# A copy in PSUM and a joint addition in the second channel product, a fourth grouped block per batch, and gates ahead of other work, in a gated attention and token-and-channel mixer

## The chip, the cores and the metric

The kernel runs on one core of a Trainium2 chip. The metric is the device time of one execution in microseconds. A core has a matmul engine (TensorE, PE in the profile), a vector engine (VectorE, DVE), a scalar engine (ScalarE, ACT), GpSimd (POOL) and SyncE (SP), which here issues DMAs. [...] Each engine works through its own list of instructions in the order in which the kernel emitted it, and semaphores order the engines against each other.

## The reference

There are 8 batches, 3008 positions (S), 256 channels, 64 columns of z, 256 token-mixing and 1536 channel-mixing hidden units:

```
attn = relu(z zT / S)^2
x    = u * (attn v)
xt   = x transposed (channels x positions)
h    = relu(xt w_tok1) w_tok2
u2   = x + h transposed
out  = u2 + relu(u2 w_ch1) w_ch2
```

All is given and returned in f32; the kernel multiplies in bf16 and accumulates in f32.

## The kernel before

A batch is cut into NQ = 6 blocks of 512 positions (the last has 448). For each block the attention half computes scores (`sc`, L470), relu and square on ScalarE and VectorE, and the product with v (`acc`, L697), which uses half of the rows of the matmul array and takes two accumulators per block half. `finish` (L809) combines them: ScalarE copies one accumulator to `cp` (L825), VectorE adds the other (L831), and `gate` multiplies with u (L851, and L856 for the last 64 positions of the short block) and writes `xT`. The buffers of the tag "res" (three) hold `cp` among others.

The mixer half of a batch has token mixing (`a_ps`, L1058, then `h_ps`, L1128), the residual, the first channel product and the second. The first channel product of a block makes twelve hidden tiles of 128 units; ordinarily each takes two matmuls of 512 columns (`hp`, L1192), and a ReLU of two tiles at once (L1231, 1024 columns). In some blocks the first four hidden tiles come in a seven-product form of a 2 x 2 block product (Strassen and Winograd's), `grouped_ch1` (L1288), in four steps a, b, c, d of 2, 2, 2 and 1 products. It needs sums of quarters of the tokens (`token_quarters`, L1256) and uses one PSUM bank pair `gp`. After step a ScalarE keeps one bank in `s5` (L1323) and copies the other bank over it (L1320); b accumulates on both; after it come a ReLU of half the tile and a second copy; after c VectorE adds both banks to `s5` in one custom instruction (L1338); after d a last ReLU. `grouped` (L1249) says which blocks: those with q of 1 to 3 in batches 1 to 7.

The second channel product of a block is also in seven-product form, `product` (L1421): products k = 1 to 7 of twelve 128-column matmuls each (six in the short last block of a batch), over tiles of hidden units and sums of them (`hsum`, L1383 to L1401). Before the change product 1 and then 6, 7 and 4 go to one bank of the pair `xb`, and 2, 5 and 3 to the banks of a second pair `zb`. Products 2, 6, 7, 4 and 3 go on top of an earlier one where the form asks for it. After each product VectorE adds the bank, with the residual `u_sb` where a quarter of the result opens, to the result tile `ro` (L1480): seven additions of 128 x 256 per block. The very last block of the kernel takes the plain form (`ch2`).

The order of all this work is written out when the kernel is built. The work alternates between attention stages and mixer stages, since attention uses half of the array's rows and the rest uses all of them; mixer stage j holds blocks 3 to 5 of one batch and 0 to 2 of the next. Within a mixer stage the pieces of a block stand in a written order: a tuple such as `GROUPED` (L1024), `ORDER_LAST` (L1026) or the plain one at L1673, where a letter is a step of the next block's group, a number other than 0 a product, and 0 the next ordinary piece of the first channel product. A planner (`next_piece`, L1690; `run_engines`, L388; `push`, L369) walks along these orders, keeps an estimated time for each engine, and emits each engine's operations when, by its estimate, they are ready. `push(engine, ready, busy, latency, ...)` puts an operation into an engine's waiting list, `room` and `needs` hold it back until buffers or other operations are there, and `first` ranks it.

Of the kernel before, what the change touches and what calls it, by code (L numbers as in the profile page):

```python
# [26 lines left out]
class Sooner:  # L27
# [5 lines left out]
    @property  # L33
    def t(self):
        return None if self.done.t is None else self.done.t - self.us


# [21 lines left out]
def kernel(  # L59
# [749 lines left out]
    def finish(blk, dh, end):  # L809


        W, acc = blk.W, blk.acc[dh]
        summed = Done()
        guess[blk.home[dh]] = end + 1.7
        ring.append((summed, blk.home[dh]))

        def load(e):
            return max(free[e], end) + sum(op.busy for op in waiting[e])

        on_act = blk.b > 0 or load("act") + 0.46 < load("dve") + 0.67  # L820

        def copy(t):
            cp = sb.tile([P, QW], F32, tag="res", name="cp", bufs=3)
            if on_act:
                nc.scalar.copy(cp[:, :W], acc[:, 1, :W])  # L825
            else:
                nc.vector.tensor_copy(cp[:, :W], acc[:, 1, :W])
            push("dve", t, 0.66, 0.78, lambda t: add(cp, t), first=1, done=summed)

        def add(cp, t):  # L830
            nc.vector.tensor_add(cp[:, :W], acc[:, 0, :W], cp[:, :W])  # L831
# [7 lines left out]
    gated = [0]  # L839

    def gate(blk, dh, acc, t):
        b, q, W = blk.b, blk.q, blk.W
        uT = uTs[b, q]
# [179 lines left out]
    BORROW = 3  # L1023
    GROUPED = ("a", 0, 1, 2, "b", 6, 5, 0, "c", 7, 3, 0, 4, "d")  # L1024
    VERY_LAST = (B - 1, NQ - 1, CHT // 2 - 1)
    ORDER_LAST = ((1, 2, 6, 5, 7, 0, 3, 4), (1, 2, 6, 5, 0, 7, 3, 0, 4))  # L1026

    def add_mixer(b):
# [150 lines left out]
        def ch1(q, c2, borrowed, end):  # L1179
# [48 lines left out]
            def evacuate(t):  # L1228
# [12 lines left out]
            engine, busy = ("act", 0.92) if on_act else ("dve", 1.15)  # L1241
# [12 lines left out]
        g_done = {(q, d, k): Done() for q in range(NQ) for d in range(CHT // 4) for k in range(3)}  # L1254

        def token_quarters(q):  # L1256
# [5 lines left out]
            def first_two(t):  # L1262
                live["xT"] += 2
                tile_["T"] = sb.tile(
                    [P, 4, 2 * P], BF16, tag="xT", name="t_sums", bufs=ROOM["xT"])
                st["T", q] = tile_["T"]
                st["s5", q] = sb.tile([P, QW], F32, tag="xT", name="s5", bufs=ROOM["xT"])
                nc.vector.tensor_sub(tile_["T"][:, 0:2], quarter[:, :, 1], quarter[:, 0])
                push("dve", t - 0.1, 0.27, 0.4, third)
# [10 lines left out]
            def begin(t):  # L1280
                push("dve", t, 0.4, 0.53, first_two, room=lambda: live["xT"] < ROOM["xT"] - 1)

# [5 lines left out]
        def grouped_ch1(q, d, stage, end):  # L1288
# [41 lines left out]
            def relu_last(t):  # L1330
                nc.scalar.activation(h[:, 1, 0], half(1), ACT.Relu)  # L1331
                recent[0] = h[:, 1, 0, :1]
                live["xT"] -= 2
                if ("rest", q, d) in st:
                    st.pop(("rest", q, d))(t)
# [79 lines left out]
        def bank_of(q, k):  # L1415

            if k in (2, 5, 3):
                return st["zb", q][:, int(k != 2)]
            return st["xb", q][:, 0]

        def product(q, k, end):  # L1421
# [6 lines left out]
            if k == 2:  # L1428
                st["z_slot", q], _ = take_slot()
                st["zb", q] = bank_pair(st["z_slot", q], "zb")  # L1430
# [20 lines left out]
            if k == 4:  # L1451
                done_with_h2(q)
                for d in range(CHT // 4):
                    release(home_of(q), [1], end + 0.2)
            collect(q, k, end)

        def collect(q, k, end):
# [9 lines left out]
            def us(m, h):  # L1467
                return st["u", q][:, h, m * n:m * n + n, :]

            blocks_of = {1: (0, 0), 2: (0, 0), 5: (1, 1), 6: (1, 0), 3: (1, 0), 7: (1, 1),  # L1470
                         4: (0, 1)}
            opening = k in (1, 5, 6, 4)

            def add(t):
                if k == 1:
# [3 lines left out]
                m, h = blocks_of[k]  # L1479
                nc.vector.tensor_add(  # L1480
                    res(m, h), source, us(m, h) if opening else res(m, h))
                recent[0] = st["res", q][:, 0, :1]
                over[q] -= 1
# [8 lines left out]
            done = taken[q, k]  # L1492
            if k == 1:
                with_u(q, ready, lambda at: push(
                    "dve", at, busy, busy + 0.15, add, first=1, room=(home_of(q),),
                    frees=frees_of(q), done=done))
            else:
                done = push("dve", ready, busy, busy + 0.15, add, first=1, done=taken[q, k],
                            room=lambda: ("res", q) in st)
            if k == 3:  # L1500
# [3 lines left out]

        over = [7] * NQ
        us_uses = [[1] for _ in range(NQ)]
# [134 lines left out]
        def add_product(q, k):  # L1641
            needs = {
                1: [Sooner(h2_done[q, c], 0.111 * c) for c in range(CHT // 2)] + w_done[2:],
                2: [], 5: [mix_done, taken[q, 2]], 6: [taken[q, 1]], 3: [taken[q, 5]], 7: [taken[q, 6]],
                4: [taken[q, 7]]}[k]
            kind = {5: 0, 7: 1, 6: 2, 4: 3}.get(k)
            if kind is not None:
                needs = needs + [Sooner(s_done[q, d, kind], 0.222 * d) for d in range(CHT // 4)]
            if q == NQ - 1 and k == 5 and b % 2 == 0:
                needs = needs + [tok1_over[b + 1]]  # L1650
            cost = pairs_of(q) * (CHT // 2) * column_time(P)
            tails.append(Piece(cost, needs, lambda end: product(q, k, end), opens=k == 1,
                               closes=k == 4, key=(b, 2 + q), slot=k in (1, 2),
                               joins=k == 1 and q == NQ - 1))
# [8 lines left out]
        for q in range(NQ):  # L1663
# [5 lines left out]
            if fast(q):  # L1669
                us_uses[q][0] += bool(rest)  # L1670
                h2_uses[q] += bool(rest)
                for k in (ORDER_LAST[b % 2] if q == NQ - 1 else GROUPED if grouped(q + 1) else
                          (0, 0, 1, 2, 0, 6, 5, 0, 7, 3, 0, 4)):  # L1673
                    if isinstance(k, str):
# [415 lines left out]
```

## Time and profile before

| | us |
|---|---|
| median of 3 runs | 1110.19 |
| the runs | 1110.31, 1108.81, 1110.19 |
| the profiled execution | 1109.13 |
| its span, first to last instruction | 1107.3 |

| engine | busy us | instructions |
|---|---|---|
| TensorE, matmuls | 1102.2 | 11199 |
| VectorE | 811.5 | 1791 |
| ScalarE | 684.7 | 906 |
| GpSimd | 168.2 | 386 |

The granted TensorE clock is 1.000 over the whole span. In the timeline a row gives the start in us from the span's start, the length in us, the engine, the line, the operation with out<-in, the shape and how many instructions it covers. Matmuls are pipelined: the printed end of a row lies behind the start of the next, so lengths of matmul work are read from start to start. In the grouped rows the number behind "x" is the count, then the busy time in us and the mean length in ns, and then the idle time of that engine just before them and what ended it.

The stage borders, by the matmuls of the timeline, are at 127.3 (mixer), 164.8 (attention), 198.3 (mixer), 267.3 (attention), 335.2 (mixer), 403.5 (attention), 471.4 (mixer), and so on with mixer stages beginning at 606.2, 742.5, 877.5 and 1011.3.

### The profile page before, as it was taken

How to read it: one execution, taken by the hardware profiler on the slowest of the kernel's cores; microseconds unless marked ns; L12 is line 12 of the kernel's file. 1: busy time of each engine (PE TensorE's matmuls, PEld its weight loads, DVE VectorE, ACT ScalarE, POOL GpSimd, SP SyncE). 2: the span in 40 equal slices, each digit the busy share in tenths (PEclk: the TensorE clock that was granted, in tenths of full speed). 3: DMA queues.
4: the chain of work that ended last, by engine and by line, in shares of the span. 5: the costliest groups of instructions: out<-in, count | busy, mean ns of one | idle time of the engine just before them, and what ended most of it. 6: DMA issues, size and time to landing. Idle time of an engine off the chain costs nothing.

```text
span 1107.3 us, 27459 instructions
## 1 busy us (share of the span) xinstructions
PE 1102.2 (100%) x11199; PEld 695.2 (63%) x11199; DVE 811.5 (73%) x1791; ACT 684.7 (62%) x906; POOL 168.2 (15%) x386
## 2 busy tenths in 40 slices
PE   9999999999999999999999999999999999999998
PEld 3444575776557665576656865557755677556776
DVE  6889865886758866578766796567966778656785
ACT  7999555646854567546665467663776537743464
POOL 5320110321003110032100320003210120000100
PEclk9999999999999999999999999999999999999999
DMA  9999947798978969789896796977989778684222
GB/s 179 167 199 184 149 96 152 127 179 146 190 127 149 190 133 177 127 156 191 140 189 120 133 218 141 170 122 150 198 160 169 116 145 185 125 160 104 64 59 96
DMA packets 465726, 165.55 MB, mean 150 GB/s; under 512 B 433024, under 2 KB 448960, under 8 KB 465600
## 3 DMA queue, kind: packets, MB, share of 16 engines
q1 hardware_dynamic: 436208, 131.11, 58.9%
q0 software_dynamic: 28880, 32.32, 21.5%
q8 instruction: 87, 1.43, 0.6%
q14 instruction: 39, 0.32, 0.1%
q10 hardware_dynamic: 512, 0.38, 0.1%
HBM read 65.40 MB, written 24.64 MB: 81 GB/s over the span
## 4 chain that ended last, share of the span: by engine, by line
PE 99%; DVE 0%; ACT 0%; issue 0%
PE acc L697 42%; PE hp L1192 19%; PE xb L1447 11%; PE zb L1447 8%; PE sc L470 6%; PE h_ps L1128 4%; PE a_ps L1058 3%; PE gp L1312 3%; PE op L1544 2%; PE first_acc L614 1%; PE wp L210 0%; DVE at L516 0%; ACT at L508 0%; DVE zr L183 0%; PE first_acc L189 0%; DVE zT L1850 0%
## 5 line engine op out<-in xcount | busy, mean ns | idle before, releaser
L697 PEld LDWEIGHTS <-v_sb 64*128 64x128 bf16 x4418 | 245.7, 94 | 212.5 <-issue 1.3
L1231 ACT ACTIVATE h2pre<-hp 128x1024 bf16<-128x1024 f32 (+1 forms) x245 | 239.9, 1005 | 182.7 <-PE hp L1192 180.5
L697 PE MATMUL acc<-at,v_sb 64*128 64x512 bf16 (+1 forms) x2738 | 341.6, 374 | 0.0
L508 ACT ACTIVATE at<-sc 128x1024 bf16<-128x1024 f32 (+1 forms) x290 | 286.8, 1027 | 72.0 <-PE sc L470 66.4
L516 DVE TENSOR_TENSOR at<-at 128x1024 bf16<-128x1024 bf16 (+1 forms) x290 | 198.1, 687 | 112.1 <-ACT at L508 107.9
L1192 PE MATMUL hp<-xT,w_ch_sb 128*128 128x512 bf16 (+1 forms) x984 | 238.3, 374 | 0.0
L697 PE MATMUL acc<-fl,v_sb 64*128 64x512 bf16 (+1 forms) x1680 | 193.0, 367 | 0.0
L1192 PEld LDWEIGHTS <-w_ch_sb 128*128 128x128 bf16 x984 | 90.8, 98 | 79.0 <-issue 2.6
L1447 PEld LDWEIGHTS <-hsum 128*128 128x128 bf16 x2088 | 127.9, 98 | 19.6 <-issue 0.5
L470 PE MATMUL sc<-zT 64*128 64x512 bf16 (+1 forms) x732 | 132.4, 359 | 0.1
L1383 DVE TENSOR_TENSOR hsum<-h2pre 128x1024 bf16<-128x1024 bf16 (+1 forms) x141 | 90.0, 647 | 22.7 <-ACT h2pre L1231 12.6
L825 ACT COPY cp<-acc 128x512 f32<-128x512 f32 (+1 forms) x94 | 54.9, 584 | 79.9 <-PE acc L697 69.0
L831 DVE TENSOR_TENSOR cp<-acc,cp 128x512 f32<-128x512 f32 (+1 forms) x94 | 63.4, 675 | 54.8 <-ACT cp L825 54.0
L1447 PEld LDWEIGHTS <-h2pre 128*128 128x128 bf16 x1566 | 93.8, 98 | 10.0
L496 ACT ACTIVATE at<-sc 128x512 bf16<-128x512 f32 (+3 forms) x152 | 56.2, 450 | 29.2 <-PE sc L470 28.8
L1447 PE MATMUL xb<-shared_sb,hsum 128*128 128x128 bf16 x1044 | 73.6, 219 | 0.0
L1480 DVE TENSOR_TENSOR ro<-xb,u_sb 128x256 f32<-128x256 f32 (+1 forms) x141 | 56.3, 400 | 17.9 <-PE xb L1447 17.7
L470 PEld LDWEIGHTS <-zT 64*128 64x128 bf16 x732 | 42.4, 94 | 41.6 <-issue 3.8
L129 POOL CAST mark<-at 128x1 f32<-128x1 bf16 x24 | 9.3, 386 | 388.1 <-DVE at L516 388.1
L851 DVE TENSOR_TENSOR xT<-cp,uT 128x512 bf16<-128x512 f32 (+1 forms) x94 | 62.4, 663 | 0.8
L547 DVE TENSOR_TENSOR at<-at 128x512 bf16<-128x512 bf16 (+3 forms) x152 | 41.0, 320 | 23.8 <-ACT at L496 23.8
L1401 DVE TENSOR_TENSOR hsum<-h2pre,hsum 128x512 bf16<-128x512 bf16 (+1 forms) x141 | 55.1, 400 | 4.1 <-ACT h2pre L1331 2.5
(107 smaller groups left out, 1114.8 us busy)
## 6 DMA issues: line engine op xcount, KB each, us to landing
out_dram<-ro SPq DMA_DIRECT2D x40, 512.0 KB, 3.2
v_sb<-in_v_dram POOLq DMA_DIRECT2D x40, 256.0 KB, 4.6
ur<-in_u_dram POOLq DMA_DIRECT2D x40, 256.0 KB, 5.0
w_tok_sb<-in_moe_w_tok_dram POOLq DMA_DIRECT2D x10, 256.0 KB, 10.5
shared_sb<-in_z_dram POOLq DMA_DIRECT2D x35, 64.0 KB, 4.2
at<-at SPq DMA_TRANSPOSE x114, 2.4
out_dram<-ro SPq DMA_DIRECT2D x7, 256.0 KB, 3.7
fl<-at SPq DMA_TRANSPOSE x105, 4.5
```

Of the source, the lines that this page charges most:

```text
L470: nc.tensor.matmul(sc[:, r, c0:c1], zT[h, k:k + P], zT[h, m + c0:m + c1], start=True, stop=True)
L496: nc.scalar.activation(a3[:, i, c0:c1], sc[:, r, c0:c1], ACT.Relu, scale=inv_S)
L508: nc.scalar.activation(view, sv, ACT.Relu, scale=inv_S)
L516: nc.vector.tensor_mul(view, view, view)
L697: nc.tensor.matmul(o, vs[blk.b, g][rows, i, dh * P:(dh + 1) * P], rhs, start=(dh, h) not in blk.begun, stop=stop, skip_group_check=True)
L831: nc.vector.tensor_add(cp[:, :W], acc[:, 0, :W], cp[:, :W])
L851: nc.vector.tensor_mul(xT[:, dh, :full * P].rearrange("p (t s) -> p t s", s=P), acc[:, :full * P].rearrange("p (t s) -> p t s", s=P), uT[: ...
L1192: nc.tensor.matmul(hps[r % len(hps)][:, r, :W], w_ch1_sb[:, dc, cc * P:(cc + 1) * P], xT[:, dc, :W], start=(dc == 0), stop=(dc == DT - 1))
L1231: nc.scalar.activation(h2[:, :, :W], hp[:, :, :W], ACT.Relu)
L1383: nc.vector.tensor_sub(sums["s"][:, 0:2, :, :n * P], h[:, :, 1], h[:, 0])
L1447: nc.tensor.matmul(to[:, i * P:(i + 1) * P], lhs, weights[:, c2, :], start=(first_use and c2 == 0 and i == 0), stop=(c2 == CHT // 2 - 1), ...
L1480: nc.vector.tensor_add(res(m, h), source, us(m, h) if opening else res(m, h))
```

## The change

There are three parts.

1. In the second channel product, product 1 now goes to bank 1 of `xb`, and ScalarE copies this bank to bank 0 (a new `fork`). Product 2 accumulates on bank 0, and 6, 7 and 4 accumulate on bank 1, so both quarters of the result that take product 1 have it in PSUM. The pair `zb` is taken at product 5 and holds only 5 and 3. VectorE adds after 5, 6, 7 and 3 as before, and after 4 once for both banks of `xb` with the residual, so a block has five additions, the last twice as wide. Product 2 now needs the copy, and the planner is told to put it behind the additions of 6 and 7; the written orders are changed to match.
2. `grouped` holds for one more block, q = 4, in batches 1 to 6. Its token sums and `s5` cannot lie in an `xT` buffer, so they share one of the six buffers of `h2`; they are made during block 3 of the mixer stage before (`LATE_T`), and lie there over the attention stage that comes between. The mixer stage that then follows opens with step a of this group, product 1 of block 3, an ordinary piece, step b. `GROUPED` becomes one order per block.
3. `gate` is ranked 0.12 us earlier in the planner's list, and the copies of the accumulators are counted, so that at most three buffers of "res" are planned as held. One estimate, that of the ReLU on ScalarE (`RELU`), is 0.95 for 0.92.

By the order of instructions there are 84 more `gp` matmuls of 256 columns and 48 fewer `hp` matmuls of 512; 47 more copies on ScalarE; 62 fewer instructions on VectorE; 18 of the 198 ReLUs of 1024 columns leave ScalarE, six of which go to VectorE. GpSimd and SyncE keep their instructions, and the DMAs stay as they are.

```diff
@@ finish / gate
         def copy(t):
+            copies[0] += 1
             cp = sb.tile([P, QW], F32, tag="res", name="cp", bufs=3)
...
-            push("dve", t, 0.58, 0.7, lambda t: gate(blk, dh, cp, t), first=1,
+            push("dve", t - 0.12, 0.58, 0.7, lambda t: gate(blk, dh, cp, t), first=1,
...
-        push(engine, end + 0.21, busy, busy + 0.15, copy, first=1)
+        push(engine, end + 0.21, busy, busy + 0.15, copy, first=1,
+             room=lambda: copies[0] + live["us"] < 3)
...
     def gate(blk, dh, acc, t):
+        copies[0] -= not blk.whole
@@ orders
-    GROUPED = ("a", 0, 1, 2, "b", 6, 5, 0, "c", 7, 3, 0, 4, "d")
+    LATE_T = 4
+    RELU = 0.95
+    GROUPED = (('a', 0, 1, 0, 'b', 2, 6, 5, 'c', 7, 3, 0, 'd', 4), ('a', 0, 1, 0, 'b', 2, 6, 5, 'c', 7, 3, 0, 'd', 4), (0, 'a', 0, 1, 0, 'b', 2, 6, 5, 'c', 7, 3, 0, 'd', 4), ('a', 1, 0, 'b', 6, 0, 5, 'c', 2, 3, 7, 'd', 0, 4), ('a', 0, 1, 0, 'b', 6, 2, 5, 'c', 7, 0, 3, 'd', 4), ('a', 0, 1, 0, 'b', 6, 2, 5, 'c', 7, 0, 3, 'd', 4), ('a', 0, 1, 0, 'b', 6, 2, 5, 'c', 7, 0, 3, 'd', 4))
+    PLAIN = (0, 1, 0, 5, 2, 6, 0, 0, 7, 0, 3, 4)
-    ORDER_LAST = ((1, 2, 6, 5, 7, 0, 3, 4), (1, 2, 6, 5, 0, 7, 3, 0, 4))
+    ORDER_LAST = ((1, 2, 6, 5, 7, 0, 3, 4), (1, 6, 0, 5, 2, 0, 3, 7, 4))
@@ the group
-            if c2 == (3 if q else 0) and q + 1 < NQ and grouped(q + 1):
+            if c2 == (0, 3, 3, LATE_T if b < B - 1 else 3)[min(q, HALF)] and q + 1 < NQ and grouped(q + 1):
                 token_quarters(q + 1)
...
-            return b > 0 and 0 < q <= HALF and d == 0
+            return b > 0 and 0 < q <= HALF + (b < B - 1) and d == 0
...
+                else:
+                    live["h2"] += 1
+                    kept = sb.tile([P, 2, QW], F32, tag="h2", name="t_s5", bufs=ROOM["h2"])
+                    tile_["T"] = kept[:, 0].bitcast(BF16).rearrange("p (k n) -> p k n", k=4)
+                    st["s5", q] = kept[:, 1]
@@ the products
-            if k in (2, 5, 3):
-                return st["zb", q][:, int(k != 2)]
-            return st["xb", q][:, 0]
+            if k in (5, 3):
+                return st["zb", q][:, 0]
+            return st["xb", q][:, int(k != 2)]
...
-            first_use = k in (1, 2, 5)
+            first_use = k in (1, 5)
...
+            if k in (2, 6, 7, 4):
+                behind = [taken[q, j] for j in (1, 6, 7)]
+                for op in waiting["dve"]:
+                    if op.done in behind:
+                        op.ready = max(op.ready, end + 0.21)
...
+            def fork(t):
+                nc.scalar.copy(bank_of(q, 2)[:, :n * P], bank_of(q, 1)[:, :n * P])
...
+                if k == 4:
+                    nc.vector.tensor_add(
+                        st["res", q][:, :n, :].rearrange("p i (h d) -> p h i d", d=P),
+                        st["xb", q][:, :, :n * P].rearrange("p h (i d) -> p h i d", d=P),
+                        st["u", q][:, :, :n, :])
+                else:
+                    m, h = blocks_of[k]
+                    nc.vector.tensor_add(
+                        res(m, h), source, us(m, h) if k in (5, 6) else res(m, h))
...
             if k == 1:
+                push("act", ready, busy, busy + 0.15, fork, first=2, done=done)
+            elif k == 2:
+                pass
+            elif begins:
...
-        over = [7] * NQ
+        over = [5] * NQ
@@ needs
-                2: [], 5: [mix_done, taken[q, 2]], 6: [taken[q, 1]], 3: [taken[q, 5]], 7: [taken[q, 6]],
+                2: [taken[q, 1]], 5: [mix_done], 6: [taken[q, 1]], 3: [taken[q, 5]], 7: [taken[q, 6]],
                 4: [taken[q, 7]]}[k]
+            if k == 2:
+                needs = needs + [Read(taken[q, j]) for j in (6, 7)]
```

More of the change, by code (lines that the diff above doesn't have):

```diff
@@ L35, in t, with __init__ @@
         return None if self.done.t is None else self.done.t - self.us
+class Read:
+    def __init__(self, done):
+        self.done = done
+    @property
+    def t(self):
+        return self.done.t or 0.0
 class Op:
@@ L1497, in collect @@
             else:
-                done = push("dve", ready, busy, busy + 0.15, add, first=1, done=taken[q, k],
-                            room=lambda: ("res", q) in st)
+                us_ = busy if k != 4 else 0.62 if n == 2 else 0.34
+                push("dve", ready, us_, us_ + 0.15, add, first=1, done=done,
+                     room=lambda: ("res", q) in st)
             if k == 3:
@@ L1671, in add_mixer @@
                 h2_uses[q] += bool(rest)
-                for k in (ORDER_LAST[b % 2] if q == NQ - 1 else GROUPED if grouped(q + 1) else
-                          (0, 0, 1, 2, 0, 6, 5, 0, 7, 3, 0, 4)):
+                for k in (ORDER_LAST[b % 2] if q == NQ - 1 else GROUPED[q + (b == B - 1) * (HALF + 1)] if grouped(q + 1) else
+                          PLAIN):
                     if isinstance(k, str):
```

44 lines of the change are left out of this document (26 added, 18 removed).

## The prediction

> **What bounds the kernel now.** I read the page's busy shares and its chain first, then TensorE's own waits, then a table of three stages, then single stretches of the timeline.
>
> ```profile
> span 1107.3 us, 27459 instructions
> PE 1102.2 (100%) x11199; PEld 695.2 (63%) x11199; DVE 811.5 (73%) x1791; ACT 684.7 (62%) x906; POOL 168.2 (15%) x386
> PE 99%; DVE 0%; ACT 0%; issue 0%
> ```
>
> ```profile
> PE wp L210 <- DVE zero L1735: 1.2, 1, 1.2
> PE first_acc L614 <- DVE at L516: 0.4, 1, 0.4
> ```
>
> ```profile
> 335.15:403.49 68.34, 68.34 (x759) 50.94 (x758) 56.74 (x142) 37.61 (x47) 17.04 (x40) 1.00 0.86 159
> 403.49:471.37 67.88, 67.88 (x650) 35.82 (x649) 41.64 (x83) 44.22 (x67) 3.81 (x9) 1.00 0.84 150
> 471.37:538.31 66.94, 66.94 (x747) 49.82 (x746) 55.92 (x138) 37.61 (x47) 18.34 (x43) 1.00 0.89 164
> ```
>
> TensorE is busy for the whole span and is 99% of the chain; the only waits listed for it are at the start. The three windows are a mixer stage, an attention stage and a mixer stage (columns: length, then busy time and instructions of PE, weight loads, DVE, ACT, POOL; granted clock; DMA share). In a mixer stage VectorE has some 11 us to spare and ScalarE some 30, the clock is 1.00, and the DMA engines carry nothing new in this change. So time goes only where matmul columns go or where TensorE is made to wait, and a wait of 0.1 us does not show as idle: it must be read from the distance between matmuls.
>
> **The change part by part.**
>
> *The extra group.* Six more blocks (one in each of batches 1 to 6) make their first four hidden tiles in the seven-product form: eight matmuls of 512 columns go, fourteen of 256 come.
>
> ```profile
> 471.37 2.76 PE L1192 MATMUL hp<-xT,w_ch_sb 128*128 128x512 bf16 x12
> 473.97 0.83 PE L1447 MATMUL xb<-w_ch_sb,h2pre 128*128 128x128 bf16 x12
> 474.64 0.83 PE L1447 MATMUL zb<-w_ch_sb,h2pre 128*128 128x128 bf16 x12
> ```
>
> ```profile
> 375.15 0.38 PE L1312 MATMUL gp<-xT,w_ch_sb 128*128 128x256 bf16 x2
> 375.37 0.38 PE L1312 MATMUL gp<-t_sums,shared_sb 128*128 128x256 bf16 x2
> 375.59 1.03 PE L1192 MATMUL hp<-xT,w_ch_sb 128*128 128x512 bf16 x4
> 376.45 0.83 PE L1447 MATMUL xb<-w_ch_sb,h2pre 128*128 128x128 bf16 x12
> ...
> 377.79 0.38 PE L1312 MATMUL gp<-xT,w_ch_sb 128*128 128x256 bf16 x2
> 378.01 0.38 PE L1312 MATMUL gp<-t_sums,shared_sb 128*128 128x256 bf16 x2
> 378.32 0.83 PE L1447 MATMUL xb<-shared_sb,hsum 128*128 128x128 bf16 x12
> ```
>
> I go by the distance of starts, since printed ends overlap the next row. Twelve 512-column matmuls take 473.97 − 471.37 = 2.60, so 0.217 each; four of 256 columns take 375.59 − 375.15 = 0.44, so 0.110 each; a product of twelve takes 474.64 − 473.97 = 0.67. A group saves 8 × 0.217 − 14 × 0.110 = 1.73 − 1.54 = 0.19 us, and six of them **−1.2 us**. This is the only matmul time that the change removes: products, token mixing and attention keep their counts.
>
> *What the group adds beside TensorE.*
>
> ```profile
> L1231 ACT ACTIVATE h2pre<-hp 128x1024 bf16<-128x1024 f32 x198 | 198.5, 1026 | 146.7 <-PE hp L1192 145.6 <-issue 1.1
> L1480 DVE TENSOR_TENSOR ro<-xb,u_sb 128x256 f32<-128x256 f32 x120 | 50.3, 419 | 12.1 <-PE xb L1447 11.9
> L831 DVE TENSOR_TENSOR cp<-acc,cp 128x512 f32<-128x512 f32 x78 | 53.5, 686 | 47.5 <-ACT cp L825 46.9
> L1338 DVE CUSTOM_DVE_ANT_1 h2pre<-gp,s 128x1024 bf16<-128x1024 f32 x21 | 25.7, 1225 | 12.0 <-PE gp L1312 12.0
> L1320 ACT COPY gp<-gp 128x512 f32<-128x512 f32 x42 | 23.9, 570 | 1.3
> L1327 ACT ACTIVATE h2pre<-gp 128x512 bf16<-128x512 f32 x21 | 12.5, 597 | 1.5
> L1268 DVE TENSOR_TENSOR t_sums<-xT 128x512 bf16<-128x512 bf16 x21 | 8.7, 416 | 0.0
> L1078 ACT COPY a_f<-a_ps 128x128 f32<-128x128 f32 x8 | 2.1, 265 | 33.7 <-PE a_ps L1058 33.7
> ```
>
> Per mixer stage VectorE gets 1.2 for the double addition, about 1.0 for the token sums (0.42 and two of some 0.3) and a ReLU of 1024 columns that the plan moves over from ScalarE, about 1.2: +3.4. ScalarE gets five of 0.57 to 0.60 (keep, two forks, two ReLUs of half a tile), 2.9 in all, less three ReLUs of 1.03 (two that the group replaces and the one moved): about 0. Nothing of this ends a chain while the 11 and 30 us are there, so I cost it at nothing; were the cover gone, each microsecond would cost one.
>
> *Product one copied, one addition of two banks.* Per block VectorE goes from seven additions of 0.42 to four and one over 512 columns, taken as the 0.69 of the L831 row: 2.93 − 2.37 = 0.56 less, 3.4 per stage, which cancels what the group brings. ScalarE gets 47 copies. A copy of 256 columns from PSUM to PSUM is not in the trace: it lies between 0.265 (128 columns, L1078) and 0.570 (512, L1320); linear in columns gives 0.37, and six per stage add 2.2, so ScalarE goes from 37.6 to about 39.8 of 68.3. What matters is when each copy ends, since product 2 writes on top of it and product 6 into the bank that it reads. Behind product 1 the written order leaves four 512-column matmuls and a group step (0.87 + 0.44 = 1.31) in grouped blocks, four matmuls and product 5 (0.87 + 0.67 = 1.54) in plain ones, and about 0.8 in the short last block of a batch. Against 0.37 and a step of a few hundredths to start, it fits unless ScalarE is inside another instruction. I take 0; the bounds are 0 and the cost of rival C.
>
> [...]
>
> *The wait of product 6.* In the rows above two pairs of 256 columns from 377.79 should end at 378.23, but the next product starts at 378.32: 0.09 lost, because the product's bank waited for VectorE's addition (L1480). That addition is gone and the order puts other work there. I see this in three stages: **−0.3 us**; bounds 0 and −0.6 (all six).
>
> *The first step of a mixer stage.* Now it opens with twelve 512-column matmuls (row 471.37). Afterwards it opens with group step a (0.44), product 1 (0.67), four 512-column matmuls (0.87), then step b, which accumulates into banks that ScalarE must have saved and copied (keep, then fork). So b is due 1.98 after the stage begins. ScalarE is in order, and ahead of keep stands the second copy of the last attention block.
>
> ```profile
> 469.96 0.53 ACT L825 COPY cp<-acc 128x448 f32<-128x448 f32 x1 [1.25 <-PE acc L697]
> 472.22 0.53 ACT L825 COPY cp<-acc 128x448 f32<-128x448 f32 x1 [1.73 <-DVE xT L856]
> 472.65 2.86 ACT L1231 ACTIVATE h2pre<-hp 128x1024 bf16<-128x1024 f32 x3
> ```
>
> ```profile
> 469.58 0.42 DVE L1388 TENSOR_TENSOR hsum<-h2pre,hsum 128x512 bf16<-128x512 bf16 x1
> 470.04 0.42 DVE L1401 TENSOR_TENSOR hsum<-h2pre,hsum 128x512 bf16<-128x512 bf16 x1
> 470.38 0.42 DVE L926 TENSOR_TENSOR d_pair<-x_pair 128x512 bf16<-128x512 bf16 x1
> 470.71 0.62 DVE L831 TENSOR_TENSOR cp<-acc,cp 128x448 f32<-128x448 f32 x1
> 471.25 0.28 DVE L926 TENSOR_TENSOR d_pair<-x_pair,d_pair 128x256 bf16<-128x256 bf16 x1
> 471.45 0.55 DVE L851 TENSOR_TENSOR xT<-cp,uT 128x384 bf16<-128x384 f32 x1
> 471.92 0.22 DVE L856 TENSOR_TENSOR xT<-cp,uT 128x64 bf16<-128x64 f32 x1
> 472.79 0.62 DVE L831 TENSOR_TENSOR cp<-acc,cp 128x448 f32<-128x448 f32 x1 [0.65 <-ACT cp L825]
> ```
>
> ```profile
> 376.35 0.61 ACT L1323 COPY s<-gp 128x512 f32<-128x512 f32 x1
> 376.99 0.57 ACT L1320 COPY gp<-gp 128x512 f32<-128x512 f32 x1
> ```
>
> The second copy sat 1.73 us for the gate of the first half (L856): both halves' copies take the same buffer, and before and after it still waits for that gate. In the new order the gate directly follows its addition, and one sum (L1388) stands ahead of the two where three instructions stood. The first copy ends at 470.49, so the addition starts at 470.55 instead of 470.71; the gate reads its result, so it starts at 470.55 + 0.62 + 0.03 (the gap between keep and fork below) = 471.20, its tail 0.47 later (471.92 − 471.45) at 471.67, done at 471.89, and ScalarE's copy 0.08 behind that (472.14 to 472.22) at 471.97 instead of 472.22. The next instruction starts 0.43 behind it (472.65 − 472.22): keep at 472.40, fork 0.64 behind keep (376.99 − 376.35) at 473.04, ended at 473.61. Step b is due at 471.37 + 1.98 = 473.35, so TensorE waits 0.27 and a few hundredths for the signal: I take 0.3, at the six stage starts that have this order, **+1.8 us**. Bounds: 0, where the copy comes 0.3 earlier; 0.6 each, 3.6 in all, where the gate brings nothing (copy at 472.22, fork's end at 473.86). I take the middle since it follows from the rows. Next late behind it would be product 6, whose bank is read by product 1's copy right after the fork; that one moves with b.
>
> The strict order of ScalarE is what makes this wait: in row 472.22 it idles 1.73 us and takes nothing from behind. [...]
>
> *Gates first* has no cost of its own: in the attention stages VectorE works 41.64 of 67.88. The waits added to the ScalarE copies hold only the planner back, not the chip.
>
> *Memory.* One of six h2 buffers holds the token sums over the attention stage; no hidden tile is made there, so no one waits for it. No DMA is added and the queues of SP and POOL keep their instructions.
>
> Sum: −1.2 − 0.3 + 1.8 = **+0.3 to +0.4**. The profiled execution took 1109.13 us, 1.1 under the median of 1110.19, so it becomes about 1109.5 and the median **1110.6 us**. 0.2% of it, 2.2 us, is about what a measurement of this kernel tells from no change: the lines are 1107.97 and 1112.41.
>
> **The rivals.**
> - A, the forecast: the wait at six stage starts eats the group's saving. 1110.6; with its bounds (stage start 0.1 to 0.55 each, product 6) 1109.3 to 1112.2. Chance 0.5.
> - B: there is no wait at the stage starts, because VectorE has less ahead of the gate or the addition starts with the copy's end. Then −1.2 − 0.3: 1108.7. For it: 0.3 us earlier is enough. Against it: every step above is from a row. Still within 0.2%. Chance 0.25.
> - C, on the other side: product 1's copies come late, because ScalarE has just begun a 1.03 us ReLU. Then the copy ends 1.03 + 0.37 + 0.05 = 1.45 behind product 1: 0.14 late in 27 grouped blocks, 0.65 late in the 7 short last blocks, nothing in the plain ones: 3.8 + 4.5 = 8.3 us at most. In half of the cases it is 4.2 us, about 1115. Beside A it decides from 1.8 us, a fifth of the cases. For it: ScalarE is 55% busy in these stages (37.61 of 68.34). Against it: the order is fixed and places the copy mostly ahead of the next ReLU. Chance 0.18.
> - D: faster by over 0.2%. It needs 2.2 us where matmul counts give 1.2; the rest would have to be waits that the trace shows only as 0.1 us here and there. Chance 0.07, mostly in the spread of the runs.
> - That the change is not carried out: in the order of instructions the 47 copies, the 84 matmuls of 256 columns and 48 fewer of 512 are all there, so no chance is set apart.
>
> **How the numbers follow.** Likeliest is A, 1110.6, its own range 1109.3 to 1112.2. Low: B's 1108.7 with 0.5 for the spread of runs, 1108.2, leaves D out. High: 1113.6 takes in C up to a third of its worst case and leaves out some 0.1. Faster 0.08 (D and B's edge), slower 0.2 (C and A's upper edge), the rest 0.72.
>
> **What would show it.** Right: 378 matmuls of 256 columns in the group, at 0.11; at 471 and its five likes, the step b pair starting some 2.3 us after the stage's first matmul instead of 1.98, released by the ScalarE fork; mixer stages otherwise of unchanged distance; VectorE's busy time in a stage near 57, ScalarE's near 40. Wrong for me: product 2 or product 6 starting late behind product 1's copy in many blocks (C), or b on time (B). The prediction also fails if a stage loses time at its end, where the plan shifted token mixing and where I found no row that prices it.

## The result, and the profile after

| | before, us | after, us |
|---|---|---|
| median of 16 runs each | 1109.09 | 1111.51 |
| lowest and highest | 1108.81, 1110.66 | 1110.98, 1115.95 |
| profiled execution | 1109.13 | 1112.42 |
| its span | 1107.3 | 1110.6 |

The ratio is 1.0023, with a 95% interval of 1.0016 to 1.0030: the changed kernel is slower by 2.4 us, at the edge of what I had called measurable. I forecast +0.4 us and 1110.6; the time lies in the range. The three runs that I had of the kernel before had a median of 1110.19; over sixteen it is 1109.09, so the forecast time fits better than the forecast difference does, and that is luck: from 1109.09 the same sum would have given 1109.5, 2.0 us under the result.

Page and TensorE's own waits of the changed kernel:

```profile
span 1110.6 us, 27562 instructions
PE 1103.2 (99%) x11235; PEld 698.6 (63%) x11235; DVE 815.2 (73%) x1727; ACT 693.9 (62%) x965; POOL 168.6 (15%) x386
PE 92%; DVE 4%; ACT 2%; DMA 1%; issue 0%; ACTq 0%
```

```profile
PE wp L221 <- DVE zero L1792: 1.2, 1, 1.2
PE sc L481 <- ACT at L519: 0.8, 1, 0.8
PE sc L481 <- DMA zT<-zr: 0.7, 1, 0.7
PE h_ps L1145 <- DVE res L1638: 0.5, 2, 0.3
```

TensorE is still nearly the whole chain, but now 7% of it runs through VectorE, ScalarE and a DMA: there are stretches in which TensorE waited for them. (These shares are the lengths of those links of the chain, not time that TensorE lost; it is busy for 99% of the span.) The list of waits names only part of these. The waits of 0.29 us below are not in it, and one of 0.42 stands as 0.26, since the end of a matmul row is drawn behind the start of the next (the row at 338.06 below ends at 338.89, the next one starts at 338.73). So I went by starts again: the distance between two rows, less what the matmuls between them take by their pitch (0.217 for 512 columns, 0.110 for 256, 0.056 for 128, 0.67 for a product of twelve).

The 0.8 on L519 is at 110.2 us in the first attention stage, where ScalarE waited 1.27 us for a DMA of `fl`. I found it in this execution and, twice as long, in one of ten others; it is most of the 0.9 us by which the profiled execution lies above its median, and I leave it out of the account below.

*The start of a mixer stage* (at 337.6 us, the first of the six; TensorE, then ScalarE):

```profile
337.61 0.39 PE L1340 MATMUL gp<-xT,w_ch_sb 128*128 128x256 bf16 x2
337.84 0.38 PE L1340 MATMUL gp<-t_s,shared_sb 128*128 128x256 bf16 x2
338.06 0.83 PE L1478 MATMUL xb<-w_ch_sb,h2pre 128*128 128x128 bf16 x12
338.73 1.03 PE L1209 MATMUL hp<-xT,w_ch_sb 128*128 128x512 bf16 x4
339.88 0.38 PE L1340 MATMUL gp<-xT,w_ch_sb 128*128 128x256 bf16 x2
```

```profile
338.21 0.53 ACT L837 COPY cp<-acc 128x448 f32<-128x448 f32 x1 [1.47 <-DVE xT L870]
338.64 0.59 ACT L1351 COPY t_s<-gp 128x512 f32<-128x512 f32 x1
339.26 0.57 ACT L1348 COPY gp<-gp 128x512 f32<-128x512 f32 x1
339.75 0.36 ACT L1512 COPY xb<-xb 128x256 f32<-128x256 f32 x1
```

Step b starts 2.27 us behind the stage's first matmul; the four ordinary matmuls ahead of it end at 338.73 + 0.87 = 339.60, so TensorE waited 0.28 to 0.29. ScalarE's copy comes 0.60, keep 1.03 and fork 1.65 behind the stage's start (forecast 0.60, 1.03 and 1.67). The six stage starts have 0.29 each.

*The start of token mixing* in the stages of odd batches. First the kernel before, then TensorE and VectorE of the changed one:

```profile
364.56 1.03 PE L1128 MATMUL h_ps<-w_tok_sb,a_f 128*128 128x512 bf16 x4
365.43 0.50 PE L1447 MATMUL xb<-w_ch_sb,hsum 128*128 128x128 bf16 x6
365.76 1.46 PE L1128 MATMUL h_ps<-w_tok_sb,a_f 128*128 128x512 bf16 x6
```

```profile
366.25 1.03 PE L1145 MATMUL h_ps<-w_tok_sb,a_f 128*128 128x512 bf16 x4
367.54 1.04 PE L1145 MATMUL h_ps<-w_tok_sb,a_f 128*128 128x512 bf16 x4 [0.26 <-DVE res L1638]
...
370.47 1.03 PE L1145 MATMUL h_ps<-w_tok_sb,a_f 128*128 128x512 bf16 x4
371.44 1.02 PE L1209 MATMUL hp<-xT,w_ch_sb 128*128 128x512 bf16 x4
```

```profile
366.01 0.29 DVE L1125 TENSOR_SCALAR a_f<-a_f 128x256 bf16<-128x256 f32 x1
366.22 0.41 DVE L1638 TENSOR_TENSOR res<-op,u_sb 128x256 f32<-128x256 f32 x1
366.55 0.20 DVE L1638 TENSOR_TENSOR res<-op,ends_lo 64x64 f32<-64x64 f32 x1
366.69 0.34 DVE L1638 TENSOR_TENSOR res<-op,ends_hi 64x192 f32<-64x192 f32 x1
367.05 0.43 DVE L1638 TENSOR_TENSOR res<-op,u_sb 64x256 f32<-64x256 f32 x1
```

In the last block of a batch a 0 of the written order stands for a piece `op` of the plain second channel product, which makes the rows that the seven-product form leaves over. Before, a product stood between the first and the second piece of token mixing and both came without a wait. Now the two follow each other, and the second waits for the additions that free the bank pair of `op` (a pair is one tile of 2 x 512 f32 columns in the kernel). Its matmuls end at 365.58, but VectorE is at the sums of `a_f` until 366.22 and only then adds `op`, in four instructions that end at 367.48. Four 512-column matmuls from 366.25 end at 367.12; the next starts at 367.54: 0.42 lost. A second wait of 0.10 stands at 371.44 (370.47 + 0.87 = 371.34). The other two odd stages lose 0.52 as well (one splits the 0.42 in 0.23 and 0.18), 1.56 in all.

The other engines did about as forecast: in this stage VectorE is busy for 56.5 us (forecast near 57) and ScalarE for 38.3 (forecast 39.8). The new copy, the joint addition, and a mixer stage of the changed kernel (columns as in the prediction):

```profile
L1512 ACT COPY xb<-xb 128x256 f32<-128x256 f32 x40 | 15.0, 374 | 0.0
L1524 DVE TENSOR_TENSOR ro<-xb,u_sb 128x512 f32<-128x512 f32 x40 | 27.2, 681 | 0.2 <-PE xb L1478 0.2
```

```profile
337.61:406.05 68.44, 68.06 (x758) 51.25 (x757) 56.51 (x132) 38.30 (x55) 16.25 (x38) 1.00 0.88 162
```

*The first attention stage* has two new waits: 0.20 at 86.4 us, and 0.22 in these rows (eight such matmuls, on half of the array's rows, take 0.86 to 0.87 from start to start where nothing waits):

```profile
99.74 1.04 PE L708 MATMUL acc<-at,v_sb 64*128 64x512 bf16 x8
100.82 0.39 PE L481 MATMUL sc<-zT 64*128 64x512 bf16 x2
```

The account, from the distances of starts in the two profiled executions:

| step | forecast, us | in the traces, us |
|---|---|---|
| fewer matmul columns (six groups) | -1.2 | -1.2 |
| step b at six stage starts | +1.8 | +1.7 |
| wait of product 6, gone | -0.3 | -0.3 |
| token mixing in three odd stages | 0, no row found | +1.6 |
| first attention stage, two places | 0 | +0.4 |
| product 1 in the first stage of batch 1 | 0 | +0.1 |
| sum | +0.4 | +2.4 |

Smaller waits that came or went elsewhere cancel to within 0.1 us.

### The profile page after: what moved, and what is told of

Its sections match the earlier page's. It is cut to its first block, busy times and chain, and to the rows that moved or that the text cites. A ratio compares the mean times of both kernels' runs of the same rounds, so it can differ in the third digit from the quotient of the medians.

```text
span 1110.6 us, 27562 instructions
## 1 busy us (share of the span) xinstructions
PE 1103.2 (99%) x11235; PEld 698.6 (63%) x11235; DVE 815.2 (73%) x1727; ACT 693.9 (62%) x965; POOL 168.6 (15%) x386
## 4 chain that ended last, share of the span: by engine, by line
PE 92%; DVE 4%; ACT 2%; DMA 1%; issue 0%; ACTq 0%
PE acc L708 38%; PE hp L1209 17%; PE xb L1478 13%; PE sc L481 6%; PE zb L1478 5%; PE h_ps L1145 4%; PE gp L1340 4%; PE a_ps L1075 3%; DVE at L527 1%; PE op L1599 1%; PE first_acc L625 1%; ACT at L519 1%; DMA fl<-at 1%; DVE hsum L1414 1%; DVE cp L843 1%; DMA zT<-zr 1%
## 5 line engine op out<-in xcount | busy, mean ns | idle before, releaser
L519 ACT ACTIVATE at<-sc 128x1024 bf16<-128x1024 f32 (+1 forms) x290 | 287.0, 1027 | 76.5 <-PE sc L481 69.8
L1248 ACT ACTIVATE h2pre<-hp 128x1024 bf16<-128x1024 f32 (+1 forms) x227 | 222.7, 1004 | 163.1 <-PE hp L1209 162.4
L1209 PE MATMUL hp<-xT,w_ch_sb 128*128 128x512 bf16 (+1 forms) x936 | 227.1, 374 | 0.0
L1209 PEld LDWEIGHTS <-w_ch_sb 128*128 128x128 bf16 x936 | 86.2, 98 | 72.4 <-issue 1.4
L1478 PEld LDWEIGHTS <-h2pre 128*128 128x128 bf16 x1566 | 97.1, 98 | 12.6
L1478 PE MATMUL xb<-w_ch_sb,h2pre 128*128 128x128 bf16 x1044 | 74.6, 219 | 0.0
L140 POOL CAST mark<-at 128x1 f32<-128x1 bf16 x29 | 12.0, 414 | 399.7 <-DVE at L527 399.7
L1432 DVE TENSOR_TENSOR hsum<-h2pre,hsum 128x512 bf16<-128x512 bf16 (+1 forms) x141 | 54.7, 400 | 2.4
L1419 DVE TENSOR_TENSOR hsum<-h2pre,hsum 128x512 bf16<-128x512 bf16 (+1 forms) x141 | 55.2, 401 | 1.7
```

Of the source, the lines that this page charges most:

```text
L519: nc.scalar.activation(view, sv, ACT.Relu, scale=inv_S)
L1209: nc.tensor.matmul(hps[r % len(hps)][:, r, :W], w_ch1_sb[:, dc, cc * P:(cc + 1) * P], xT[:, dc, :W], start=(dc == 0), stop=(dc == DT - 1))
L1248: nc.scalar.activation(h2[:, :, :W], hp[:, :, :W], ACT.Relu)
L1419: nc.vector.tensor_sub(kind(2), quarters(q, d)[:, 1, 1], kind(0))
L1478: nc.tensor.matmul(to[:, i * P:(i + 1) * P], lhs, weights[:, c2, :], start=(first_use and c2 == 0 and i == 0), stop=(c2 == CHT // 2 - 1), ...
```

## The experiments

Each kernel is compared with runs of the kernel before on the same chip; the medians of these were 1109.09 to 1109.84, so the ratio is the safer number. Against it the changed kernel has 1.0023. The diffs show the lines, or the parts of long lines, that change; the changed tuple of `GROUPED` is that of block 3, that of `ORDER_LAST` the one for odd batches.

**Old written order of the last block in odd batches.**

```diff
-    ORDER_LAST = ((1, 2, 6, 5, 7, 0, 3, 4), (1, 6, 0, 5, 2, 0, 3, 7, 4))
+    ORDER_LAST = ((1, 2, 6, 5, 7, 0, 3, 4), (1, 2, 6, 5, 0, 7, 3, 0, 4))
```

> The changed kernel with the old written order of the last block in odd batches, (1, 2, 6, 5, 0, 7, 3, 0, 4). Theory: in the three mixer stages concerned TensorE waits about 0.5 us at the start of the second token mixing (0.42 or 0.23 + 0.18 before its second piece, 0.10 later), because the pair of banks of the ordinary piece comes free late; with the old order these waits go (a 0.19 wait that the old order has elsewhere in these stages may stay), so 1.0 to 1.5 us less than the changed kernel, about 1110.2 against 1109.1 before. Rival (the loss lies in product one's copies or in the first attention stage): no difference beyond 0.3 us.

Measured: 1110.36 us, ratio 1.0010 (1.0001 to 1.0019), so 1.4 us less than the changed kernel by the ratios (1.2 by the medians). In the trace the 1.56 us of token mixing are gone and the stage starts keep their 0.29:

```profile
365.63 1.47 PE L1599 MATMUL op<-w_ch_sb,hs 128*128 128x256 bf16 x12
366.94 1.03 PE L1145 MATMUL h_ps<-w_tok_sb,a_f 128*128 128x512 bf16 x4
367.81 0.50 PE L1478 MATMUL xb<-w_ch_sb,hsum 128*128 128x128 bf16 x6
368.14 1.89 PE L1145 MATMUL h_ps<-w_tok_sb,a_f 128*128 128x512 bf16 x8
```

A product stands between the token pieces again and no wait is left there. That a written order of products in one block, and not the copies, made this loss is shown.

**The second accumulator copy behind the group's copies on ScalarE.**

```diff
-        push(engine, end + 0.21, busy, busy + 0.15, copy, first=1,
+        late = 1.0 * (blk.q == NQ - 1 and dh == 1 and blk.b > 1)
+        push(engine, end + 0.21 + late, busy, busy + 0.15, copy, first=1,
```

> The changed kernel with the second accumulator copy of the last attention block placed behind keep, the fork of the group and the copy of product one on ScalarE. Theory: the six waits of 0.29 us ahead of step b at the stage starts go, -1.7 us, 1109.8, unless the bank pair of that accumulator, which now comes free over 1 us later, is what the next piece waits for. Rival (step b waits for something else, such as the double-buffered banks or VectorE): the six waits stay, 1111.5.

Measured: 1113.3 us, ratio 1.0034 (1.0022 to 1.0047). All six waits of step b are gone, which shows that they came from ScalarE's order. But the wait moved:

```profile
339.32 0.38 PE L1341 MATMUL gp<-xT,w_ch_sb 128*128 128x256 bf16 x2
339.54 0.38 PE L1341 MATMUL gp<-t_s,shared_sb 128*128 128x256 bf16 x2
339.76 0.83 PE L1479 MATMUL xb<-shared_sb,hsum 128*128 128x128 bf16 x12
340.78 1.02 PE L1210 MATMUL hp<-xT,w_ch_sb 128*128 128x512 bf16 x4 [0.19 <-DVE cp L843]
```

Step b stands at its due time, 1.98 behind the start (337.34). The next ordinary piece is due at 339.76 + 0.67 = 340.43 and starts at 340.78, 0.35 late, because the accumulator's bank pair comes free only behind the late copy (339.35 to 339.90) and its addition. The exception that the expectation named was the case. Over the six stages 2.25 us are lost there in place of 1.73, and in one stage step d and product 4 lose another 0.75, behind a VectorE instruction that waited 0.78 for a DMA. How much of the measured 1.2 us (by the ratios) such events make in other executions was not seen.

**Without the extra group.**

```diff
-            return b > 0 and 0 < q <= HALF + (b < B - 1) and d == 0
+            return b > 0 and 0 < q <= HALF and d == 0
```

> The changed kernel without the extra group of block 4 in batches 1 to 6. Theory: the matmuls cost 1.2 us more and the six waits of 0.29 go, so -0.5 us: 1111.0; the waits in token mixing of odd batches stay. Rival (the group is worth its 1.2 us and the loss is elsewhere): +1.2, 1112.7.

Measured: 1111.35 us, ratio 1.0018 (1.0009 to 1.0026): 0.5 us less than the changed kernel by the ratios, as expected, though the intervals overlap and the times alone would not tell it from nothing. In the trace the b waits are gone and token mixing keeps its 1.6. So by the traces the group, as it is placed, loses half a microsecond: 1.7 of waits against 1.2 of columns.

**Both of the first two.**

```diff
-        push(engine, end + 0.21, busy, busy + 0.15, copy, first=1,
+        late = 1.0 * (blk.q == NQ - 1 and dh == 1 and blk.b > 1)
+        push(engine, end + 0.21 + late, busy, busy + 0.15, copy, first=1,
...
-(1, 6, 0, 5, 2, 0, 3, 7, 4))
+(1, 2, 6, 5, 0, 7, 3, 0, 4))
```

> Both: the second copy late and the old order of the last block. Theory: the two losses add up, -1.7 and -1.0 to -1.5, so 1108.3 to 1108.8, just under the kernel before (1109.1). If they don't add up, one of them was cover for the other.

Measured: 1110.89 us, ratio 1.0013 (1.0004 to 1.0022). A miss, for the reason that the second experiment gives: the late copy brings nothing, the old order brings its 1.6 less what the late copy costs. The profiled execution took 1114.21, 3.3 above the median, and shows what else a late copy risks (VectorE, then TensorE):

```profile
748.86 0.43 DVE L941 TENSOR_TENSOR d_pair<-x_pair 128x512 bf16<-128x512 bf16 x1 [1.61 <-DMA x_pair<-xT]
```

```profile
750.27 1.87 PE L1210 MATMUL hp<-xT,w_ch_sb 128*128 128x512 bf16 x4 [2.88 <-DVE cp L843]
```

The accumulator's addition stood behind a sum that waited for a DMA, and TensorE lost 3.05 us at one place. The granted clock was 0.59 from 750.2 to 754.0, and 512-column matmuls came 0.39 to 0.43 apart in place of 0.217, by my estimate about 1.5 us more (3.8 us at 0.59). The mean clock of this execution is 0.998; why it was lower in this stretch was not shown.

**The gate ranked as before.**

```diff
-            push("dve", t - 0.12, 0.58, 0.7, lambda t: gate(blk, dh, cp, t), first=1,
+            push("dve", t, 0.58, 0.7, lambda t: gate(blk, dh, cp, t), first=1,
```

> The changed kernel with the gate ranked as before (no 0.12 us lead). Theory: at the six stage starts a sum goes back between the addition and the gate, the second copy comes later by 0.25 and step b waits some 0.55 instead of 0.29: +1.5; in the first attention stage the order of the kernel before returns and its two new waits (0.20 and 0.22) go: -0.4. Together +1.1 against the changed kernel's 1111.5: 1112.6. Rival (the gate's rank changes nothing at the stage starts): the b waits stay at 0.29 and the time is 1111.1.

Measured: 1113.05 us, ratio 1.0029 (1.0018 to 1.0040), between 0.7 (by ratios) and 1.5 us (by medians) more than the changed kernel. The trace gives 1.3: 1.25 more at the stage starts, 0.42 less in the first attention stage, 0.48 more at product 1. At the first of the six stage starts, ScalarE then TensorE:

```profile
337.82 0.53 ACT L837 COPY cp<-acc 128x448 f32<-128x448 f32 x1 [1.68 <-DVE xT L870]
```

```profile
337.01 0.39 PE L1340 MATMUL gp<-xT,w_ch_sb 128*128 128x256 bf16 x2
...
339.49 0.38 PE L1340 MATMUL gp<-xT,w_ch_sb 128*128 128x256 bf16 x2 [0.33 <-ACT gp L1348]
```

The copy comes 0.81 behind the stage's start and not 0.60, step b 2.48 and not 2.27: it waits 0.50 where the forecast said 0.55, and the releaser is the group's fork on ScalarE. The two waits of the first attention stage go, as expected. A third place was not foreseen: product 1 in the first mixer stage of batch 1 waits 0.62 (0.14 in the changed kernel), since the ReLUs that it needs stand behind a late copy there too. (The eighth experiment, with the same gate, shows the row.)

**Step b later, a second ordinary piece ahead of it.**

```diff
-('a', 1, 0, 'b', 6, 0, 5, 'c', 2, 3, 7, 'd', 0, 4)
+('a', 1, 0, 0, 'b', 6, 5, 2, 'c', 3, 7, 'd', 0, 4)
```

> The changed kernel with the order of block 3 as a, 1, 0, 0, b, 6, 5, 2, c, 3, 7, d, 0, 4: a second ordinary piece stands ahead of step b, which is due 2.84 us behind the stage's start and not 1.98. Theory: keep and fork are done at 2.24, the six waits of 0.29 go and nothing takes their place, since step c comes 2.0 behind b: -1.7, 1109.8. Rival (ScalarE is so full behind the stage's start that step c or product 2 becomes the late one): waits of some tenths ahead of c or 2, 1111 or more.

Measured: 1115.34 us, ratio 1.0054 (1.0041 to 1.0066). A miss of 5.5 us. TensorE's waits:

```profile
PE xb L1478 <- DVE ro L1530: 1.8, 5, 0.5
PE gp L1340 <- DVE h2pre L1369: 1.5, 5, 0.3
```

Step b is on time, but product 2 now comes too early behind 6: in five of the six stages it waits 0.5 to 0.6 for VectorE's addition of 6, which reads the other bank of the same pair and stands behind five sums of pairs (1.76 us in the first of these stages), and step d, with two products ahead of it where three stood, waits up to 0.5 for VectorE's double addition. Over the six stages that is 2.7 and 2.6 us. The rival had one of the two places right (product 2); the engine is VectorE.

**Three menders at once: that order, the old last order, and the gate's lead only from batch 2 on.**

```diff
-('a', 1, 0, 'b', 6, 0, 5, 'c', 2, 3, 7, 'd', 0, 4)
+('a', 1, 0, 0, 'b', 6, 5, 2, 'c', 3, 7, 'd', 0, 4)
...
-(1, 6, 0, 5, 2, 0, 3, 7, 4))
+(1, 2, 6, 5, 0, 7, 3, 0, 4))
...
-            push("dve", t - 0.12, 0.58, 0.7,
+            push("dve", t - 0.12 * (blk.b > 1), 0.58, 0.7,
```

> The changed kernel with three things mended: the order of block 3 of the last run, the old order of the last block in odd batches, and the gate's lead kept for batches 2 to 7 only, so that the first attention stage keeps its old order. Theory: -1.7, -1.5 and -0.4 add up, to 1107.9, which would be 0.1 to 0.15% under the kernel before (1109.1 to 1109.6). Rival (the waits cover for each other): 1109 or more.

Measured: 1113.65 us, ratio 1.0035 (1.0023 to 1.0048). It carries the waits of the last run and is 1.7 us under it, which is about the old last order again. The gate's part comes to nothing: the two waits of the first attention stage are gone, and product 1 of batch 1 waits 0.62 again.

**The copy and the joint addition alone.**

```diff
-            return b > 0 and 0 < q <= HALF + (b < B - 1) and d == 0
+            return b > 0 and 0 < q <= HALF and d == 0
...
-(1, 6, 0, 5, 2, 0, 3, 7, 4))
+(1, 2, 6, 5, 0, 7, 3, 0, 4))
...
-            push("dve", t - 0.12, 0.58, 0.7,
+            push("dve", t, 0.58, 0.7,
...
-             room=lambda: copies[0] + live["us"] < 3)
+             )
```

> The copy of product one and the joint addition alone: no extra group, gates and room as before, the last block in its old order. Theory: product one's copies are in time everywhere, the wait of product 6 (0.09 in three stages) is gone and one or two waits of 0.1 come: 0 to -0.3 against the kernel before, no difference that can be told. Rival C of the prediction (copies late behind a ReLU in a fifth of the blocks or more): 2 us slower or more, and waits ahead of products 2 or 6 of xb.

This run keeps the new written orders of the other blocks, which go with the copy, and the new value of `RELU`. Measured: 1110.17 us, ratio 1.0005 (0.9996 to 1.0014): no difference that can be told. No product waits for a copy of product 1. The one new wait of a fixed place is that of product 1 in batch 1 (TensorE, then ScalarE):

```profile
202.97 0.28 PE L1478 MATMUL xb<-w_ch_sb,h2pre 128*128 128x128 bf16 x2 [0.45 <-ACT h2pre L1248]
```

```profile
199.62 0.53 ACT L837 COPY cp<-acc 128x448 f32<-128x448 f32 x1 [0.60 <-DVE xT L870]
```

By starts the wait is 0.62 (202.97 − 201.79 − 10 × 0.056). The second copy waits for the gate there too, and everything behind it on ScalarE with it. But it did so in the kernel before as well (ScalarE, then TensorE):

```profile
199.63 0.53 ACT L825 COPY cp<-acc 128x448 f32<-128x448 f32 x1 [0.60 <-DVE xT L856]
```

```profile
198.34 4.49 PE L1192 MATMUL hp<-xT,w_ch_sb 128*128 128x512 bf16 x20
```

There five ordinary pieces stood ahead of product 1, and now four do. So what uncovers this wait is the written order, which puts product 1 one piece (0.87 us) earlier, and not the copy that the change adds.

**Product 5 ahead of step b, three products left between c and d; old last order.**

```diff
-('a', 1, 0, 'b', 6, 0, 5, 'c', 2, 3, 7, 'd', 0, 4)
+('a', 1, 0, 5, 'b', 6, 0, 'c', 2, 3, 7, 'd', 0, 4)
...
-(1, 6, 0, 5, 2, 0, 3, 7, 4))
+(1, 2, 6, 5, 0, 7, 3, 0, 4))
```

> The changed kernel with the old order of the last block in odd batches and with block 3 ordered a, 1, 0, 5, b, 6, 0, c, 2, 3, 7, d, 0, 4: product 5, which waits for nothing that is made in this stage, stands ahead of step b, which is due 2.64 us behind the stage's start; three products stay between c and d, product 2 stays behind c. Theory: by ScalarE's rows of the changed kernel keep and fork end at 2.22 and the second fork at 4.5, when step c is due at 4.6, so the six waits of 0.29 go and at most some 0.05 comes ahead of d: -1.5 against 1110.4 of the run with the old last order alone, about 1108.9, level with the kernel before or just under it. Rival (another wait takes their place, as in the runs before): 1110 or more.

Measured: 1109.25 us against 1109.84 for the kernel before, ratio 0.9992 (0.9982 to 1.0002): 3.4 us under the changed kernel by the ratios, and level with the kernel before. The traces account for 2.3 of the 3.4. Step b is on time:

```profile
336.18 0.39 PE L1340 MATMUL gp<-xT,w_ch_sb 128*128 128x256 bf16 x2
...
338.16 0.83 PE L1478 MATMUL zb<-shared_sb,hsum 128*128 128x128 bf16 x12
338.83 0.38 PE L1340 MATMUL gp<-xT,w_ch_sb 128*128 128x256 bf16 x2
```

It starts 2.65 behind the stage's first matmul, directly behind product 5. What came instead is 0.05 ahead of step d, as expected, and 0.19 ahead of product 4 in four stages and 0.10 in a fifth, 0.85 us that I had not foreseen; there TensorE waits for VectorE's addition of product 7.

**Every copy of product one done twice.**

```diff
                 nc.scalar.copy(bank_of(q, 2)[:, :n * P], bank_of(q, 1)[:, :n * P])
+                nc.scalar.copy(bank_of(q, 2)[:, :n * P], bank_of(q, 1)[:, :n * P])
```

> The changed kernel with each of the 47 copies of product one done twice in a row, so that it ends about 0.27 us later and ScalarE has 13 us more work. Theory (the copies have 0.3 us or more of room in most blocks, ScalarE is far from full): a few waits ahead of products 2 and 6, the stage starts' product 6 among them (six of some 0.1 to 0.2), together 0.5 to 2 us more, 1112 to 1113.5. Rival C of the prediction (the copies are already on the edge): nearly the whole 0.27 in most blocks, 8 us or more.

Measured: 1113.24 us, ratio 1.0025 (1.0012 to 1.0038); the ratio is 0.2 us above that of the changed kernel, the medians against before differ by 1.0. The trace shows where a later copy is felt:

```profile
339.23 0.38 PE L1340 MATMUL gp<-t_s,shared_sb 128*128 128x256 bf16 x2
339.68 0.83 PE L1478 MATMUL xb<-shared_sb,hsum 128*128 128x128 bf16 x12
```

Product 6 waits 0.45 - 0.22 = 0.23 at each of the six stage starts, 1.4 us in all, and no product of any other block waits for its copy. So elsewhere the copies have more room than the second copy takes (it starts 0.40 behind the first, at 339.27 and 338.87).

Not tried: a buffer of its own for the second accumulator copy, so the wait for the gate was not taken away by itself.

## Why the prediction was right or wrong

- **What bounds the kernel.** Right, and the method (distances of starts) was the one needed after the change too.
- **The group's columns**, -1.2: right.
- **The stage starts**, +1.8: right in place, size and cause; the steps on ScalarE were forecast to 0.02 us. Taking the copy out of the way removed the waits (second experiment), putting a sum back in front of the gate raised them to 0.50 (fifth), giving step b 0.67 us more removed them (ninth). That ScalarE keeps its order could not be read from row 472.22, where no work behind the copy was ready (the four matmuls of the next ReLU end at 471.37 + 0.87 = 472.24). The runs show it: with the copy behind, keep starts 337.99 − 337.34 = 0.65 behind the stage's start (second), and in the fifth ScalarE idles past that point, to 0.81, and takes the copy first. Rival B is refuted: step b was late at all six.
- **Gates first.** My sentence that it "has no cost of its own" was half wrong. At the stage starts it is worth 0.2 us each and at product 1 of batch 1 another 0.5; but it also reordered the first attention stage, where two waits of 0.20 and 0.22 are new; with the old rank they are gone (fifth). I looked at VectorE's load there and not at the order.
- **Product 1's copies**, 0: right. The copy took 0.374 (forecast 0.37), and rival C is refuted: alone, the copies change nothing that can be told (eighth), and done twice they are late only at the six stage starts (tenth).
- **Product 6's wait**, -0.3: right.
- **The step that failed** is the last sentence of the prediction, on token mixing: I named the place (though at the end of a stage, while the loss stands in its middle, some 30 us behind its start) and entered 0 for lack of a row. It was 1.56 us, nearly all of the error of 2.0. The rows were there. In the kernel before, the two pieces of `op` and two half-size products lie between the last matmul of the first token product (to 361.27) and token mixing (364.56), 3.29 us, in which VectorE finishes the sums of `a_f` and then waits for `op`. The new order moves one piece of `op` ahead and a half-size product in, and leaves 2.31 us (363.94 to 366.25): the sums of `a_f` end behind `op`, the additions of `op` begin 0.64 behind its end (0.20 in the kernel before), and with no product between the two pieces of token mixing nothing covers it. The first experiment shows that this order alone makes the loss; its two sides were not tried apart. My estimate from the rows is that either would do: additions 0.44 earlier would leave nothing of the 0.42, and a half-size product (0.33) between the two pieces would leave 0.09.
- Since that term was left out, I gave "within 0.2%" too much weight and "slower" too little; the result is at that line. Counted from the median that I had, rival A's own upper bound was 2.0 us slower, and 2.4 were measured: by difference the result lies in the part of the range that I kept for rival C, whose mechanism did not occur. That the time lies inside A's own bounds comes from the high median of the three runs, which is luck.

## What to carry to other kernels

When TensorE is the bound, a change that takes columns away is worth only what its new dependencies leave of it: here 1.7 us of waits stood against 1.2 us of columns. Write down for each accumulating step when it is due and when the engine that it needs can have reached it, counting what stands ahead of it in that engine's list and what that waits for (here a copy that waited 1.47 us for a gate at a stage's start). Do this at every place where an order was rewritten, above all where pieces that share a small ring of buffers come to stand side by side; a place without a row in the old trace is a term of unknown size, not of size zero (here 1.56 us). And a fix that moves one engine's instruction back can free the step in front and delay the buffer behind (in the second experiment a wait of 0.29 went and one of 0.35 came): look for who takes that buffer next.

## What the runs showed that I had not expected

The joint addition holds both banks of `xb` until VectorE reaches it (in the execution below from 394.34, where the row behind product 4 starts, to 396.97), and this makes the end of a block sensitive to output writes. In several executions of the variants (not in those shown above of before and after) a group step waited for it, 0.05 to 0.95 us, at one place, in one execution at two. The longest, from the run without the extra group, TensorE then VectorE:

```profile
397.02 0.38 PE L1340 MATMUL gp<-xT,w_ch_sb 128*128 128x256 bf16 x2 [0.79 <-DVE ro L1524]
```

```profile
395.68 0.69 DVE L1414 TENSOR_TENSOR hsum<-h2pre 128x1024 bf16<-128x1024 bf16 x1 [1.64 <-DMA out_dram<-ro]
396.29 0.68 DVE L1524 TENSOR_TENSOR ro<-xb,u_sb 128x512 f32<-128x512 f32 x1
```

A sum waited 1.64 us for an earlier output write to free its buffer, the joint addition stood behind it in VectorE's order, and the group's first step behind that. The lengths seen go from 0.05 to 0.95 us; how much of the median such waits make, the runs don't tell.
